# A planned attention and gated MLP kernel: the normalization goes from either of two engines to VectorE alone, and the instruction lists are searched anew under another rule for the shared port

## The chip, the cores and the metric

The kernel runs on one core of one Trainium2 chip. A core has five engines that run beside each other, each through its own list of instructions in order: TensorE (PE in the rows; its weight loads are PEld), VectorE (DVE), ScalarE (ACT), GpSimd (POOL) and SyncE (SP), which here issues the transfers. They wait for each other on semaphores. The metric is the device time of one execution in microseconds.

## The reference

Attention with 4 sink positions and a window of 128, over 4 batches of 8 heads, 768 positions, 64 values a head; its output goes through a gated MLP that mixes positions.

```python
scores = q @ k.T / sqrt(64)                      # kept: first 4 positions, and 0 <= i - j < 128
a = softmax(scores);  x = a @ v                  # [4, 768, 512] over all heads
h = relu(x @ w_in);  u, vv = h[..., :512], h[..., 512:]
v_n = (vv - mean(vv)) / sqrt(var(vv) + 1e-6)     # over the 512 features
v_s = einsum('ts,bsd->btd', w_spatial, v_n) + b_spatial[None, :, None]
out = (u * v_s) @ w_out
```

## The kernel before

Each batch is cut into 6 tiles of 128 positions, each tile into two halves of 4 heads: 48 half tiles. A half tile goes through this sequence; the names are those of the profile's tiles, the lines those of the profile.

- TensorE makes the scores `sc` (L901); VectorE masks them into `pexp` and finds the maximum (L906); ScalarE takes the exponential (L911).
- The weights are split into two f16 numbers: a high part, a rounded copy (L609 on ScalarE, L614 on VectorE), and a low part, the difference (L625, "p low", on VectorE or GpSimd). Both are written to `p` and turned by a transposing transfer into `pT` (L975). TensorE multiplies with the values into `av` (L1017 to L1025). VectorE divides (L1031 to L1033) and `x` is split in the same way and turned into `xT`.
- The first four tiles of batch 0 are "crossed": they stay in f32 and are turned by TensorE (`pt`, L938).
- TensorE makes `ps_v` from `xT` and `w_in` (L648, crossed L1091); ScalarE takes relu into `vr` (L1104); VectorE takes the statistics (L1110 to L1114); GpSimd takes the power -1/2 of the variance (L1117, tile `rs`); and the normalization L1120, one `tensor_scalar` that subtracts the mean and multiplies by that root, runs on VectorE or GpSimd. Then `vr` is split into `vn` (high L609 or L614, low L625).
- After all tiles of a batch have `vn`, TensorE makes `ps_s` with w_spatial, VectorE gates it (L1173, L1177, L1185, tile `g`), and `ps_o` with `w_out` gives the output. `ps_u`, the other half of w_in, is made from `xT` at any time before.

The order is not written by hand. Each step is added as a piece to a `Plan` with a rank (a table `WHEN` of offsets for each kind of step), the engines that may do it with an assumed cost on each, the tiles that it reads and writes, and a flag `shared`. `Plan.order` is a list scheduler that runs while the kernel is built: it keeps a time at which each engine comes free, takes again and again the piece that could end first (ties by rank), picks the engine, and at last sorts all pieces by the start that it gave them. That sorted order is what is written into the engines' lists; on the chip only the lists and the semaphores are left. `GAP` spaces kinds of steps out. The method `beside` prices the port that VectorE and GpSimd share: pieces with `shared=True` take longer in the plan when the other engine is at work.

```python
        if e == "d" and shared:
            return d + min(d, max(free["p"] - t, 0.0))
```

Here `d` is a piece's cost, `t` its start, and `free["p"]` the time at which GpSimd comes free. Where the plan sees TensorE idle, `warm` (L550) puts matmuls without a use ahead of the next piece.

Of the kernel before, what the change touches and what calls it, by code (L numbers as in the profile page):

```python
# [13 lines left out]
ALU = mybir.AluOpType  # L14
# [199 lines left out]
def scale_from_high_word(nc, pool, top, name):  # L214
# [15 lines left out]
NS = 4  # L230
# [17 lines left out]
    "p cross": (-687.57,), "x cross": (45.68,), "x copy": (-530.15,), "pt copy": (-21.66,),  # L248
    "qk load": (-52.27, -22.45), "k sink": (-299.97, -241.1), "k copy": (596.81, -4.88), "score": (-460.83, -45.27),
    "mask": (-434.05, -132.56), "exp": (-231.67, 303.69), "p high": (441.41, -96.21), "turn high": (936.3, 182.28),  # L250
    "sink high": (86.75, 1307.65), "sink low": (617.97, -42.55), "p low": (9.93, 184.55),
    "turn low": (-277.66, 336.94), "av": (-267.85, -97.14), "divide": (-122.58, -1.13), "x high": (2.44, 222.74),
    "x low": (-647.02, -338.15), "x turn": (-365.59, 573.11), "v load": (-91.35, 1.12), "v sum": (-115.53, -183.64),
    "v max": (-417.04, -486.9), "v scale": (49.3, 574.51), "v sink": (-76.81, 48.39), "v high": (-585.85, -85.54),
    "v low": (-1194.79, 92.72), "ps_v": (-90.29, 124.42), "v relu": (447.33, 231.24), "icv": (340.13, -439.38),
    "icu": (18.96, -359.27), "v stats": (-316.16, 10.81), "v root": (-34.24, 24.3), "v norm": (43.93, 41),
    "vn high": (-784.06, -355.87), "vn low": (132.46, 27.81), "ps_u": (430.62, 636.6), "u relu": (24.49, 187.78),
    "ps_s": (111.73, -587.51), "gate": (-484.79, -130.08), "times": (64.03, 257.91), "g high": (403.16, 1442.73),
    "g low": (-262.53, 67.91), "ps_o": (-30.69, -432.82), "o copy": (502.59, -325.5), "o store": (409.39, 625.48),
    "w_in 1 load": (866.11, -447.38), "w_in 1": (-114.89, -221.77), "w_in 1 split": (308.49, 129.53),  # L260
    "w_in 0 load": (-50.92, 1059.89), "w_in 0": (157.5, -167.59), "w_in 0 split": (-824.82, 34.49),
    "w_sp load": (441.32, 71.67), "w_sp sum": (660.12, -208.54), "w_sp split": (-36.66, 542.23),
    "w_out load": (383.08, 214.87), "w_out": (194.27, 993.88), "w_out split": (-129.44, 578.24), "q 0": (-157.42,),
    "w 0": (-429.64,), "w 1": (-392.14,), "v 0": (-82.26,), "w 2": (-173.84,), "v 1": (-173.83,), "w 3": (-391.66,),
    "v 2": (-159.4,), "q 1": (-83.27,),
}
GAP = {"o": 4.275, "pace": 0.925, "pace 0": 9.634, "s": 0.598, "u": 3.332, "v sum": 0.483, "w_in 0": 13.729, "w_in 1": 10.370, "w_out": 0.000, "w_sp": 11.737}
# [23 lines left out]
class Plan:  # L291
# [213 lines left out]
def fast_path(tc, st, qk, v, vs, w_in, w_sp, b_sp, w_out, out):  # L505

    nc = tc.nc
    TC = 256
    VNS = 2.0 ** 10
    G_LOW = 11  # L510
    G_U, G_S, G_B = 2.0 ** -20, 2.0 ** -24, 2.0 ** -27
    G_WIDE = 2.0 ** G_LOW / (G_U * G_S)
    with (
# [88 lines left out]
        def high(name, step, b, kind, n, views, reads, writes, scale=None):  # L602
# [16 lines left out]
            plan.add(name, step, b, ENGINES[kind], costs(kind, n, pointer=scale is not None), f, reads, writes)  # L619
# [35 lines left out]
        vals = {}  # L655
# [31 lines left out]
        def decode(name, step, src, i, c, f0, top=None):  # L687
# [6 lines left out]
            def clamp(e):  # L694
# [12 lines left out]
                ci(), ci(), 0x07FFFFFF, 3, op0=ALU.bitwise_and, op1=ALU.logical_shift_left), [], [("w32", i)])  # L707
# [3 lines left out]
            plan.add(name, step, 0, "p", 1.22, lambda e: nc.gpsimd.tensor_tensor(  # L711
                out=ci(), in0=ci(), in1=tl("wtmp", i), op=ALU.add), [("wtmp", i)], [("w32", i)])

        def w_in_half(half):
            name, f0 = f"w_in {half}", 512 * half
            gap = GAP[name]
            key = ("in", half)
            mx = vals["mx", key] = small.tile([P, KC], F32, tag="mxw", name="mxw", bufs=3)
            for c in range(KC):
# [4 lines left out]
                ("s", key), scale_from_high_word(nc, scal, vals["r", key], f"win{half}")), 2.35)  # L724
# [591 lines left out]
```

## Time and profile before

| | us |
|---|---|
| median of 3 runs | 471.77 (469.93 to 471.91) |
| profiled execution, its own time | 468.96 |
| its span, first to last instruction | 466.9 |
| TensorE busy / VectorE busy / ScalarE busy / GpSimd busy | 427.9 / 343.6 / 223.4 / 179.6 |
| mean granted TensorE clock, share of full speed | 0.964 |

The busy times are sums over the whole span and the stages differ, so the rows below also cut the span into stretches. PEclk is the granted TensorE clock as a share of 2.4 GHz; a stretch at 1.2 GHz shows 0.5.

### The profile page before, as it was taken

Reading aid. Unit: us, or ns where it says so; the run is one execution under the profiler, and the core shown is the slowest. Engines: PE = TensorE matmul, PEld = TensorE weight load, DVE = VectorE, ACT = ScalarE, POOL = GpSimd, SP = SyncE. Lnnn points to the kernel's source line nnn. Section 1 sums busy time; section 2 is a strip of 40 time slices with the busy share of each in tenths; the row PEclk is TensorE's granted clock in tenths of the full one; section 3 lists DMA queues with packets and bytes.
Section 4 is the critical chain, followed back from the end, with each engine's and each line's share of the span. In section 5 each row is a group of like instructions: output and inputs, shape, how many; then the busy total and the mean of one; then the engine's idle time right before and its main releaser. Section 6 shows DMA issues by size and latency. Waiting matters only on the chain.

```text
span 466.9 us, 9659 instructions
## 1 busy us (share of the span) xinstructions
PE 427.9 (92%) x3571; PEld 301.0 (64%) x3571; DVE 343.6 (74%) x988; ACT 223.4 (48%) x509; POOL 179.6 (38%) x205
## 2 busy tenths in 40 slices
PE   5789999887899899898989999999799999999993
PEld 4557666654677577456567667656587867488761
DVE  4798878998798998987789737858795536366331
ACT  5797986663557746546555325434340212320110
POOL 4506438847849646522505305306830001110000
PEclk9899999987989899899999999999799999999998
DMA  6987239366989972599958034366336212400101
GB/s 253 354 254 252 69 105 239 77 162 171 203 165 187 188 184 46 160 231 188 226 115 187 36 102 114 86 155 104 75 80 93 69 46 46 90 1 0 48 31 67
DMA packets 130055, 61.39 MB, mean 131 GB/s; under 512 B 105296, under 2 KB 118352, under 8 KB 130000
## 3 DMA queue, kind: packets, MB, share of 16 engines
q1 hardware_dynamic: 129856, 60.69, 53.9%
q8 instruction: 30, 0.49, 0.5%
q14 instruction: 25, 0.20, 0.1%
q10 hardware_dynamic: 144, 0.00, 0.0%
HBM read 28.82 MB, written 6.29 MB: 75 GB/s over the span
## 4 chain that ended last, share of the span: by engine, by line
PE 47%; DVE 18%; issue 13%; POOL 12%; ACT 4%; DMA 3%; SPq 0%; POOLq 0%; ACTq 0%; DVEq 0%
PE ps_s L648 13%; PE ps_o L1200 9%; PE ps_u L648 6%; POOL vr L1120 5%; PE sc L901 5%; PE ps_v L648 5%; DVE pexp L906 2%; POOL p L625 2%; PE ps_v L1091 2%; PE av L1011 2%; DVE vn L614 2%; ACT pexp L911 2%; DVE x L625 2%; POOL rs L1117 1%; DMA out<-ob 1%
## 5 line engine op out<-in xcount | busy, mean ns | idle before, releaser
L911 ACT ACTIVATE pexp<-pexp,nm 128x260 f32<-128x260 f32 (+1 forms) x192 | 82.1, 484 | 62.5 <-DVE nm L906 62.1
L648 PE MATMUL ps_s<-wsp,vn 128*128 128x256 f16 x864 | 102.2, 276 | 4.1 <-ACT ob L1211 4.1
L648 PEld LDWEIGHTS <-vn 128*128 128x128 f16 x864 | 84.3, 99 | 20.3 <-issue 7.7
L625 POOL TENSOR_TENSOR p<-pexp,p 128x1024 f16<-128x1024 f32 (+2 forms) x45 | 61.9, 1383 | 35.1 <-ACT p L609 28.8
L648 PE MATMUL ps_u<-xT,win 128*128 128x256 f16 x576 | 69.8, 278 | 2.3 <-DVE allmax_r L676 1.4
L901 PE MATMUL sc<-kring,q 64*128 64x260 f32 (+1 forms) x384 | 62.2, 413 | 9.0 <-DVE nm L906 8.9
L1200 PE MATMUL ps_o<-wout,g 128*128 128x512 f16 x288 | 65.4, 379 | 0.7 <-DVE g L1173 0.7
L648 PEld LDWEIGHTS <-win 128*128 128x128 f16 x576 | 56.4, 100 | 14.0 <-issue 5.3
L648 PE MATMUL ps_v<-win,xT 128*128 128x512 f16 x240 | 57.3, 396 | 0.0
L901 PEld LDWEIGHTS sc<-kring,q 64*128 64x128 f32 x384 | 38.6, 195 | 23.2 <-DVE nm L906 13.4
L1117 POOL TENSOR_TENSOR rs<-rs,mhalf 128x1 f32<-128x1 f32 x24 | 16.3, 680 | 91.5 <-DVE rs L1114 89.2
L1211 ACT ACTIVATE ob<-ps_o,ico 128x512 f32<-128x512 f32 (+1 forms) x24 | 16.0, 667 | 69.7 <-PE ps_o L1200 69.6
L1200 PEld LDWEIGHTS <-g 128*128 128x128 f16 x288 | 27.8, 98 | 31.8 <-issue 1.9
L648 PEld LDWEIGHTS <-xT 128*128 128x128 f16 x240 | 23.5, 102 | 30.1 <-issue 6.3
L1173 DVE SCALAR_TENSOR_TENSOR g<-ps_s,b_bc 128x256 f32<-128x256 f32 x48 | 20.1, 419 | 28.5 <-PE ps_s L648 28.4
L1151 ACT ACTIVATE u<-ps_u 128x256 f32<-128x256 f32 x48 | 17.8, 376 | 33.5 <-PE ps_u L648 33.1
L1120 POOL TENSOR_SCALAR vr<-vr,mv,rs 128x512 f32<-128x512 f32 x14 | 31.4, 2243 | 1.1
L1023 PE MATMUL av<-vring,pT 128*128 128x65 f16 x296 | 31.8, 196 | 0.0
L1025 PE MATMUL av<-vring,pT 128*128 128x65 f16 x296 | 31.7, 196 | 0.0
L1024 PE MATMUL av<-vring,pT 128*128 128x65 f16 x296 | 31.7, 196 | 0.0
L1023 PEld LDWEIGHTS <-pT 128*128 128x128 f16 x296 | 27.9, 99 | 1.9 <-issue 0.7
L1024 PEld LDWEIGHTS <-pT 128*128 128x128 f16 x296 | 27.8, 99 | 0.9
(163 smaller groups left out, 702.0 us busy)
## 6 DMA issues: line engine op xcount, KB each, us to landing
vraw<-v_s SPq DMA_DIRECT2D x24, 260.0 KB, 4.0
kring<-qk_t SPq DMA_DIRECT2D x24, 256.0 KB, 3.7
q<-qk_t SPq DMA_DIRECT2D x24, 256.0 KB, 3.3
out<-ob SPq DMA_DIRECT2D x24, 256.0 KB, 2.2
dec<-w_in SPq DMA_DIRECT2D x8, 512.0 KB, 6.6
wsp<-w_sp_t SPq DMA_DIRECT2D x6, 384.0 KB, 5.1
dec<-w_out SPq DMA_DIRECT2D x4, 512.0 KB, 4.4
pT<-p SPq DMA_TRANSPOSE x80, 3.1
```

The lines of the kernel that those rows point to most:

```text
L625: eng[e].tensor_tensor(out=o, in0=x, in1=hi, op=ALU.subtract)
L648: nc.tensor.matmul(o, a, m, start=(i == 0), stop=(i == n - 1))
L901: nc.tensor.matmul(view(h + q)[0], tl("q", (b, t))[rows, hp, :], keys, start=True, stop=True)
L911: nc.scalar.activation(po, po, AF.Exp, bias=nm()[:, q:q + 1], scale=-1.0)
L1023: nc.tensor.matmul(o[:, h], ph, vh, start=(t < 2 and j == 0), stop=False)
L1024: nc.tensor.matmul(o[:, h], ph, vl, start=False, stop=False)
L1025: nc.tensor.matmul(o[:, h], pl, vh, start=False, stop=(j == nb - 1 and (t < 2 or h == HH - 1)))
L1117: nc.gpsimd.tensor_tensor(out=vals["rs", i], in0=vals["rs", i], in1=mhalf, op=ALU.pow)
L1120: eng[e].tensor_scalar(vr(), vr(), vals["mv", i][:, 0:1], vals["rs", i], op0=ALU.subtract, op1=ALU.mult)
L1151: plan.add("u relu", r, b, "a", 0.365, lambda e: nc.scalar.activation(tl("u", (b, c0))[:, d, :], tl("ps_u", i)[:, :TC], AF.Relu, scale=G_U ...
L1173: nc.vector.scalar_tensor_tensor(out=g(), in0=tl("ps_s", i)[:, :TC], scalar=G_S, in1=b_bc[:, t0:t0 + TC], op0=ALU.mult, op1=ALU.add)
L1200: nc.tensor.matmul(o, lead, wout[:, w, d, :], start=(d == 0 and j == 0), stop=(d == KC - 1 and j == 2))
```

## The change

`v norm` had two engines to choose from, and now has VectorE alone. Five more kinds of pieces get `shared=True` (the rounded copies, the shift of the decode, the bias, a scaled copy of w_out, the scaled copy `g high`, and the normalization itself). In `beside` a shared VectorE piece no longer pays at most its own length: it pays 0.9 of all that is left of GpSimd's current piece. A dozen assumed costs are set anew. With these, the tables `WHEN` and `GAP` are replaced whole. No instruction's shape is changed, and no data moves to another place; what differs is which engine does a piece and where it stands in its list.

```diff
 WHEN = {
-    "p cross": (-687.57,), "x cross": (45.68,), "x copy": (-530.15,), "pt copy": (-21.66,),
+    "p cross": (-463.47,), "x cross": (37.18,), "x copy": (-412.04,), "pt copy": (-12.77,), "qk load": (27.62, 80.81),
...
-GAP = {"o": 4.275, "pace": 0.925, "pace 0": 9.634, "s": 0.598, "u": 3.332, "v sum": 0.483, "w_in 0": 13.729, "w_in 1": 10.370, "w_out": 0.000, "w_sp": 11.737}
+GAP = {"o": 0.446, "pace": 0.422, "pace 0": 10.293, "s": 4.023, "u": 3.039, "v sum": 2.275, "w_in 0": 5.196, "w_in 1": 7.851, "w_out": 0.221, "w_sp": 5.631}
...
         if e == "d" and shared:
-            return d + min(d, max(free["p"] - t, 0.0))
+            return d + 0.9 * max(free["p"] - t, 0.0)
...
-            plan.add(name, step, b, ENGINES[kind], costs(kind, n, pointer=scale is not None), f, reads, writes)
+            plan.add(name, step, b, ENGINES[kind], costs(kind, n, pointer=scale is not None), f, reads, writes, shared=True)
...
-            plan.add("score", i, b, "PE", 1.16 if t else 0.7, product, [("q", (b, t))] + keys, banks)
+            plan.add("score", i, b, "PE", 1.05 if t else 0.75, product, [("q", (b, t))] + keys, banks)
...
-                plan.add("av", i, b, "PE", 0.113 * n + (0.5 if t > 1 else 0.1), product_f32,
+                plan.add("av", i, b, "PE", 0.225 * n + (0.25 if t > 1 else 0.0), product_f32,
...
-            plan.add("v root", r, b, "p", 0.5, root, [], [("st", i)])
-            plan.add("v norm", r, b, "dp", {"d": 0.46, "p": 0.66}, norm, [("st", i)], [("vr", i)])
+            plan.add("v root", r, b, "p", 0.57, root, [], [("st", i)])
+            plan.add("v norm", r, b, "d", 0.46, norm, [("st", i)], [("vr", i)], shared=True)
...
             plan.add("g high", r, b, ENGINES["g high"], costs("g high", TC), lambda e: scaled_copy(
-                e, g2()[:, 0], g(), 2.0 ** -G_LOW), [("g", i)], [("g2", i, 0)])
+                e, g2()[:, 0], g(), 2.0 ** -G_LOW), [("g", i)], [("g2", i, 0)], shared=True)
```

Three places show how the lists move. The first is GpSimd's list before, in batch 0, from the normalization of one tile to the low part of the weights (p low, `128x1024`) that stands behind the normalization of another.

```order
L1117 TENSOR_TENSOR rs<-rs,mhalf 128x1
L1120 TENSOR_SCALAR vr<-vr,mv,rs 128x512
L625 TENSOR_TENSOR p_0_133<-pexp,p_0_133 128x1024
L625 TENSOR_TENSOR p_0_133<-pexp,p_0_133 128x16
L1117 TENSOR_TENSOR rs<-rs,mhalf 128x1
L625 TENSOR_TENSOR vn<-vr,vn 128x512
L1120 TENSOR_SCALAR vr<-vr,mv,rs 128x512
L625 TENSOR_TENSOR p_1_134<-pexp,p_1_134 128x1024
```

Twice a `128x1024` subtraction is the next instruction behind a normalization. This is GpSimd's list of the changed kernel at a like place, the roots of three tiles.

```order
L1117 TENSOR_TENSOR rs<-rs,mhalf 128x1 x2
L625 TENSOR_TENSOR vn<-vr,vn 128x512
L625 TENSOR_TENSOR p_1_134<-pexp,p_1_134 128x16
L625 TENSOR_TENSOR p_1_134<-pexp,p_1_134 128x1024
L1117 TENSOR_TENSOR rs<-rs,mhalf 128x1
L1177 TENSOR_TENSOR g<-g,u 128x256
```

The normalizations are gone from it, and what follows a root is a small or a short piece. The second place is VectorE's list before, at the second of those normalizations; the first `vn` cast waits for GpSimd's normalization.

```order
L614 CAST p_1_134<-pexp 128x1024
L616 TENSOR_SCALAR vring<-vraw,v_scale 128x8x64
L614 CAST vn<-vr 128x512
L1031 TENSOR_SCALAR den<-av 128x8
L1032 RECIPROCAL den<-den 128x8
L1033 TENSOR_TENSOR x<-av,den 128x512
L625 TENSOR_TENSOR p_1_134<-pexp,p_1_134 128x16
L625 TENSOR_TENSOR vn<-vr,vn 128x512
```

This is VectorE's list of the changed kernel in batch 3, where two tiles are normalized one behind the other.

```order
L614 CAST p_0_133<-pexp 128x1024
L1110 BN_STATS st<-vr 128x6
L1112 BN_AGGR mv<-st 128x2
L1114 TENSOR_SCALAR rs<-mv 128x1
L1120 TENSOR_SCALAR vr<-vr,mv,rs 128x512 x2
L614 CAST vn<-vr 128x512 x2
L625 TENSOR_TENSOR vn<-vr,vn 128x512 x2
```

The cast `vn` now follows the normalization on its own engine. The third place is TensorE's list near the start, the crossed tiles before: scores, `av` and the first `ps_v` take turns.

```order
L901 MATMUL sc<-kring,q 128x260 x4
L1011 MATMUL av<-vraw,pT 128x65 x8
L1091 MATMUL ps_v<-w_167,xT_462 128x512
L1091 MATMUL ps_v<-w_176,xT_462 128x512
L1091 MATMUL ps_v<-w_198,xT_462 128x512
L1091 MATMUL ps_v<-w_187,xT_462 128x512
L938 MATMUL pt<-ident,pexp 128x128 x4
L901 MATMUL sc<-kring,q 128x260 x4
```

And this is the same stretch of the changed kernel, the half tiles of the crossed tiles up to the first `ps_v`.

```order
L1007 MATMUL av<-vsraw,p_0_133 128x260
L1011 MATMUL av<-vraw,pT 128x65 x8
L665 MATMUL ps_row<-ident,allmax_m 1x128
L954 MATMUL pt<-ident,p_1_134 16x128
L901 MATMUL sc<-kring,q 128x260 x4
L1007 MATMUL av<-vsraw,p_1_134 128x260
L1011 MATMUL av<-vraw,pT 128x65 x8
L672 MATMUL ps_col<-allmax_789,ones 128x1
L901 MATMUL sc<-kring,q 128x260 x4
L1091 MATMUL ps_v<-w_176,xT_599 128x512
```

The first `ps_v` stood behind the scores of the fifth half tile; it now stands behind those of the ninth, all eight crossed half tiles first. Counted over the engines' lists, GpSimd has 14 normalizations, 23 of p low at 1024 and none of `x` low before, and 0, 21 and 4 now; VectorE has 10, 11 and 20, and now 24, 13 and 16. The plan writes the pieces of all engines in one order. In it, the next VectorE piece behind a p low on GpSimd (1024 or 512 wide) is one that reads and writes SBUF alone (a rounded copy, a low part, the normalization, a `g` piece and the like) at 11 of 26 places before, and at 6 of 24 now. What stands behind the last scores on TensorE is nearly the same list as before.

## Rows read from the trace of the kernel before

**Rows 1.** Busy time by stage; the clock and transfers stand last in each row.

```profile
core 0: us, PE busy (x) PEld busy (x) DVE busy (x) ACT busy (x) POOL busy (x), PEclk, DMA share, GB/s
0.00:17.00 17.00, 9.80 (x63) 7.25 (x63) 10.42 (x37) 9.55 (x19) 9.07 (x38) 1.00 0.81 286
17.00:60.00 43.00, 40.92 (x260) 29.40 (x260) 37.17 (x137) 37.57 (x92) 16.17 (x21) 0.96 0.67 218
60.00:342.00 282.00, 259.70 (x2328) 180.15 (x2326) 234.92 (x659) 150.44 (x348) 144.85 (x135) 0.95 0.65 144
342.00:460.00 118.00, 117.48 (x926) 84.24 (x924) 60.35 (x158) 25.49 (x51) 9.50 (x12) 1.00 0.23 51
460.00:467.00 7.00, 0.00 (x0) 0.00 (x0) 0.74 (x2) 0.38 (x1) 0.00 (x0) 0.80 0.24 83
```

**Rows 2.** TensorE's waits from 60 to 342 us: total us, times, longest.

```profile
PE sc L901 <- DVE nm L906: 8.5, 7, 2.4
...
PE av L1017 <- DVE p L625: 2.4, 1, 2.4
```

**Rows 3.** TensorE in time around 124 us, with idle time and releaser.

```profile
124.35 2.14 PE L648 MATMUL ps_s<-wsp,vn 128*128 128x256 f16 x18
128.90 0.27 PE L1017 MATMUL av<-vsink,pT 96*128 96x260 f16 x1 [2.41 <-DVE p L625]
```

**Rows 4.** Busy time in two stretches around that wait, columns as in rows 1.

```profile
126.00:129.00 3.00, 0.59 (x6) 0.32 (x4) 2.93 (x6) 0.21 (x1) 1.43 (x1) 1.00 0.45 162
129.00:133.00 4.00, 4.00 (x41) 3.05 (x40) 4.00 (x14) 3.52 (x8) 0.81 (x1) 0.59 0.93 117
```

**Rows 5.** GpSimd in time, 114 to 128 us.

```profile
114.54 2.60 POOL L1120 TENSOR_SCALAR vr<-vr,mv,rs 128x512 f32<-128x512 f32 x1
...
122.65 2.75 POOL L1120 TENSOR_SCALAR vr<-vr,mv,rs 128x512 f32<-128x512 f32 x1
125.38 2.05 POOL L625 TENSOR_TENSOR p<-pexp,p 128x1024 f16<-128x1024 f32 x1
```

**Rows 6.** VectorE in time in the same stretch.

```profile
114.66 0.69 DVE L614 CAST p<-pexp 128x1024 f16<-128x1024 f32 x1
...
122.43 0.79 DVE L614 CAST p<-pexp 128x1024 f16<-128x1024 f32 x1
...
125.44 2.27 DVE L614 CAST vn<-vr 128x512 f16<-128x512 f32 x1 [1.82 <-POOL vr L1120]
...
128.67 0.17 DVE L625 TENSOR_TENSOR p<-pexp,p 128x16 f16<-128x16 f32 x1
```

**Rows 7.** The chain of waits from 60 to 342 us, shares by line.

```profile
by line: issue 20.7%; POOL vr L1120 7.6%; PE ps_s L648 6.7%; PE sc L901 5.2%; POOL p L625 3.8%; PE ps_o L1200 3.7%; DVE pexp L906 3.5%; DVE vn L614 3.3%; DVE x L625 2.6%; PE ps_v L648 2.3%; POOL rs L1117 2.2%; DMA out<-ob 2.1%; DVE vsink L8
```

**Rows 8.** By tile: count, then duration in ns, least/median/greatest.

```profile
L1120 POOL TENSOR_SCALAR vr<-vr,mv,rs x14: 2071/2078/2755, 38.4 to 332.7; 128x512 f32<-128x512 f32 x14
L614 DVE CAST vn<-vr x14: 426/526/2278, 117.2 to 413.8; 128x512 f16<-128x512 f32 x14
L1120 DVE TENSOR_SCALAR vr<-vr,mv,rs x10: 542/546/2268, 66.5 to 413.2; 128x512 f32<-128x512 f32 x10
L625 DVE TENSOR_TENSOR x<-x,x x20: 677/691/2540, 86.2 to 396.7; 128x512 f16<-128x512 f32 x20
```

**Rows 9.** Groups by line and shape: busy us, mean ns, idle before.

```profile
L625 DVE TENSOR_TENSOR x<-x,x 128x512 f16<-128x512 f32 x20 | 20.1, 1007 | 0.7 <-POOL x L618 0.4
...
L614 DVE CAST vn<-vr 128x512 f16<-128x512 f32 x14 | 14.1, 1010 | 13.3 <-POOL vr L1120 13.1
...
L625 DVE TENSOR_TENSOR p<-pexp,p 128x1024 f16<-128x1024 f32 x11 | 13.7, 1241 | 0.1
...
L616 DVE TENSOR_SCALAR vring<-vraw,v_scale 128x512 f16<-128x512 f32 x13 | 6.1, 493 | 4.1 <-PE av L1025 4.1
```

**Rows 10.** Crossed `ps_v` in the chain of waits: start, length (us).

```profile
32.44 3.49 PE ps_v L1091 x8
...
52.16 3.44 PE ps_v L1091 x8
```

More of the change, by code (lines that the diff above doesn't have):

```diff
@@ L247 @@
 WHEN = {
-    "p cross": (-687.57,), "x cross": (45.68,), "x copy": (-530.15,), "pt copy": (-21.66,),
[L249 to L262, printed above, removed]
@@ L263 @@
-    "w_out load": (383.08, 214.87), "w_out": (194.27, 993.88), "w_out split": (-129.44, 578.24), "q 0": (-157.42,),
-    "w 0": (-429.64,), "w 1": (-392.14,), "v 0": (-82.26,), "w 2": (-173.84,), "v 1": (-173.83,), "w 3": (-391.66,),
-    "v 2": (-159.4,), "q 1": (-83.27,),
+    "p cross": (-463.47,), "x cross": (37.18,), "x copy": (-412.04,), "pt copy": (-12.77,), "qk load": (27.62, 80.81),
+    "k sink": (-1265.13, 104.01), "k copy": (1027.62, 30.74), "score": (-293.87, -87.66), "mask": (-569.68, -239.03),
@@ new lines @@
+    "exp": (-634.67, 808.04), "p high": (720.35, 12.02), "turn high": (1064.07, 324.41),
+    "sink high": (-226.41, 321.96), "sink low": (1193.15, 285.79), "p low": (8.77, 523.02),
+    "turn low": (-58.83, -13.88), "av": (-442.88, -275.38), "divide": (-115.55, 272.28), "x high": (-0.1, 227.04),
+    "x low": (-660.57, -237.49), "x turn": (-483.18, 614.2), "v load": (41.52, -24.87), "v sum": (-65.63, -332.06),
+    "v max": (-330.92, -514.68), "v scale": (76.16, 725.38), "v sink": (-187.98, -157.05),
@@ new lines @@
+    "v high": (-793.18, -91.53), "v low": (-1369.63, -23.34), "ps_v": (-16.36, 369.67), "v relu": (842.89, -264.63),
+    "icv": (362.96, -678.96), "icu": (-27.18, -350.17), "v stats": (-661.98, 102.13), "v root": (63.18, -272.42),
+    "v norm": (226.43, 511.61), "vn high": (-707.79, 74.9), "vn low": (197.01, -136.51), "ps_u": (1001.89, 408.24),
+    "u relu": (168.52, 254.14), "ps_s": (162.18, -524.45), "gate": (-535.26, -88.95), "times": (199.34, 393.2),
+    "g high": (280.49, 1526.6), "g low": (-455.93, 37.4), "ps_o": (-66.37, -161.59), "o copy": (486.93, -365.12),
@@ new lines @@
+    "o store": (-207.96, 765.9), "w_in 1 load": (11.93, -684.46), "w_in 1": (-166.94, -359.53),
+    "w_in 1 split": (607.72, -344.83), "w_in 0 load": (59.71, 1218.5), "w_in 0": (167.24, 327.78),
+    "w_in 0 split": (-597.61, -151.86), "w_sp load": (169.08, 71.79), "w_sp sum": (898.55, -272.36),
+    "w_sp split": (-211.46, 256.73), "w_out load": (530.5, 325.36), "w_out": (187.77, 716.58),
+    "w_out split": (-915.03, 463.68), "q 0": (-217.71,), "w 0": (-464.18,), "w 1": (-253.4,), "v 0": (55.57,),
```

17 lines of the change are left out of this document (9 added, 8 removed).

## The prediction

> **What bounds the kernel now.** I read the busy time by stage first. From 342 to 460 us TensorE is busy for 117.48 of 118 us at the full clock, and the last 7 us are the way out of the last tile: nothing there can be had by another order, since TensorE's work stays the same. From 17 to 60 us TensorE is busy for 40.92 of 43, with ScalarE at 37.57. What is left is the stage from 60 to 342 us: TensorE works for 259.70 of 282 us, so 22.3 us are idle, and the clock's mean there is 0.95, so about 0.05 x 282 = 14 us more are lost to stretches at 1.2 GHz [rows 1]. Some 36 us are to be had at most, and the last scores fall at the end of this stage; the 125 us behind them are fixed. VectorE is the busiest of the others, 234.92 of 282 us or 83%, ScalarE 53%, GpSimd 51% [rows 1].
>
> The waits of TensorE say who is late: the largest is for VectorE's masks, 8.5 us in 7 waits [rows 2]. One stall can be followed whole. TensorE sat idle for 2.41 us before the `av` at 128.90, until VectorE's small low part at 128.67 [rows 3, 6]; in the 4 us that came next the mean clock was 0.59, which costs 4 x 0.41 = 1.6 us more [rows 4]. So a stall of this size costs about 4 us, and 36 us are some nine of them.
>
> Why VectorE was late stands two rows up. GpSimd's normalization ends at 125.40; at 125.38 by the rows, that is at once, its next instruction starts, a p low of 2.05 us. VectorE's cast of `vn` waited for that same normalization and starts at 125.44, 60 ns behind the p low [rows 5, 6]. It takes 2.27 us, where the least of these casts took 0.426 [rows 8]: it is held until p low ends. So a collision costs 2.278 - 0.426 = 1.85 us. The normalization on GpSimd thus sets up the collision: it releases VectorE's cast at the very moment at which GpSimd goes on to its next piece. The chain of waits runs over L1120 on GpSimd for 7.6% of the 282 us, 21.4 us, more than over any other engine's line [rows 7].
>
> **The change part by part.** *The normalization.* VectorE takes 14 more at the median 0.546 us, +7.6 us; GpSimd loses 14 at 2.078 us or more, at least 29 us [rows 8]. GpSimd is busy for half of the stage, so what counts there is not its time but what it blocks.
>
> Does the normalization itself hold VectorE? Beside the two that ran 2.60 and 2.75 us, VectorE's casts of `p` took 0.69 and 0.79 us; it was the normalization that got longer, from 2.07 [rows 5, 6, 8]. So nothing is to be gained from lifting it off the port, only from not releasing the cast beside a p low. The Trainium skill, page "SBUF — State Buffer", section "Who interferes with whom", says that the pair of ports which VectorE and GpSimd share is an exclusive lock, held for a whole instruction by the one that starts first. The p low agrees with it, the normalization does not; by the page alone, the 14 normalizations would free up to 14 x 2.078 = 29 us of lock, by the rows none.
>
> *Other pieces that change engine.* VectorE gets 2 more p low at 1.241 us, +2.5; it loses 4 low parts of `x` at 0.691, -2.8, and 6 scaled copies `vring` at 0.493, -3.0 [rows 8, 9]. The other kinds move by one to six pieces each and cancel to within 0.3 us by their rows in the same view. VectorE's work is then +7.6 + 2.5 - 2.8 - 3.0 = +4.3 us, nearly all of it ahead of the last scores. ScalarE gets the scaled copies and a few rounded ones; at 53% in the stage it has room, and I cost them at nothing there. If that cover is gone (it is not there before 60 us, at 87%), each costs its length.
>
> *The collisions.* The casts of `vn` paid 14 x (1.010 - 0.426) = 8.2 us for them, the low parts of `x` 20 x (1.007 - 0.677) = 6.6 us, the two costliest forms [rows 8, 9]. In the new order the places where a VectorE piece that works from SBUF alone comes directly behind a p low of GpSimd fall from 11 to 6: 5 x 1.85 = -9.3 us. Bounds: the order is one thing and the moment another, so none may go (0); at most both forms lose all that they pay, -14.8. I take -9.3, since the casts behind a GpSimd normalization are gone as a pattern. The new pattern that could replace it is a normalization on VectorE released by the root on GpSimd just as a p low follows: one of the ten before paid for that, 2.268 against 0.546 us [rows 8], and in the new GpSimd list a root is mostly followed by a small piece. VectorE's sum is then +4.3 - 9.3 = -5.0 us, with ends of +4.3 and -10.5.
>
> *The latency.* Where a normalization is on the chain, 2.078 us become 0.546: of 21.4 us at most 21.4 x (1 - 0.26) = 15.8 go [rows 7, 8]. The least is nothing, where another chain lies close beside. The root stays on GpSimd, and now a semaphore stands between it and the normalization; the cast behind it needs none across engines, so I put the exchange at nothing.
>
> *The early crossed tiles.* Two crossed `ps_v` of 3.5 us each stood in the stretch from 17 to 60 us [rows 10], and now come behind all eight half tiles. If the stretch gets shorter by that, nothing is lost. ScalarE's 37.57 of 43 us lets it shrink by 5.4 at most [rows 1]; the 1.6 us that remain of 7.0 find room in 22.3 us of later idle time. I put it at nothing, with the other end below.
>
> *Sum.* VectorE's -5.0 us and the chain's 0 to -15.8 are two views of the same stalls and are not added. I take -6, one and a half stalls of 4 us: the first figure with a little of the second, near its low end because `issue`, the masks and the transfers have their own shares in the chain [rows 7]. The profiled execution took 468.96 us of its own, 2.8 below the median of 471.77 (its span is 466.9); 468.96 - 6 = 463.0, a ratio of 0.987, and on the median 465.6. I say 465.5.
>
> **The rivals.** *More comes back.* If the casts and the normalizations were the head of most stalls, the chain's whole 15.8 us go and with them the slow clock behind: 471.77 - 16 = 456. For it: the share in the chain. Against it: the other shares.
>
> *No change.* The collisions move to other pieces: the 6 places left, and four new low parts of `x` on GpSimd, which also read two tiles. -9.3 becomes about -4.3 and cancels with the work: 471.8.
>
> *Slower, VectorE becomes the bound.* At 83% it has the least room in the stage. Its +4.3 us of work come surely, the -9.3 depend on moments. If the collisions do not fall, +4.3 and one new stall of 4 us give 480. It decides as soon as VectorE's time above its least durations falls by less than 4.3 us. The Trainium skill, page "Perfetto Trace Analysis", section "Optimizing Scalar/DVE Operations", speaks for this rival: with VectorE saturated, work may be better moved off it, GpSimd included, though it warns that the shared port may undo that. The change does the opposite.
>
> *Slower, the crossed tiles.* Without `ps_v` between them the half tiles have only their own chain (scores, mask, exponential, turn, copy, `av`). If that chain does not get faster, the stretch stays 43 us, TensorE idles 7 us more in it, and the `ps_v` are paid later: at most +7, with some filled later about +5, 477. It decides when TensorE's busy time in the first 60 us falls with no earlier ninth score.
>
> **How the numbers follow.** Chances: the forecast, 2.4 to 11 us faster, 0.42 (its own range 460.5 to 469.5); more than that 0.14; no change 0.18; VectorE the bound 0.14; the crossed tiles 0.12. A measurement of this kernel can tell about 0.5%, 2.4 us, from no change. Faster 0.42 + 0.14 = 0.56, same 0.18, slower 0.26. The range for 8 in 10 goes from 455, which leaves out the best half of the first rival, to 477, which leaves out the VectorE rival and half of the other slow one's upper side.
>
> **What would show it.** Right: the casts of `vn` on VectorE with a mean near 0.5 us instead of 1.01; VectorE's waits at p low fewer by about five; TensorE's idle time in the middle stage below 20 us and its clock above 0.95; L1120 nearly gone from the chain; and the stage behind the last scores as long as before, 118 us. Wrong: normalizations on VectorE with a mean far above 0.55 us (held by a p low behind the root), the first 60 us with less TensorE work and no gain in time, or new waits of TensorE for `pT` or `x` that make up the stalls that went.

## The result, and the profile after

The changed kernel takes 441.55 us (median of 4, 440.75 to 443.53) against 470.85 (469.84 to 471.91) for the kernel before on the same chip: a ratio of 0.938, 95% interval [0.934, 0.943], 29 us or 6.2% faster. I had said 465.5, with a range down to 455. The sign was right, the size was far off. The profiled execution has a span of 439.9 us, 27.0 less than the 466.9 of before. Runs more than 1.5% above the fastest of their kernel are left out of all ratios below, but not of the medians.

The first lines of its page give the busy time of each engine, with the share of the span and the instructions.

```profile
span 439.9 us, 9637 instructions
PE 412.7 (94%) x3569; PEld 293.1 (67%) x3569; DVE 333.4 (76%) x991; ACT 230.6 (52%) x520; POOL 146.0 (33%) x190
```

TensorE does the same products (3569 and 3571 instructions) in 412.7 us of busy time, where it took 427.9; of this 15.2 us the larger part is the slow clock: at mean clocks of 0.964 and 0.986 some 17 us of the span were lost to it before and some 6 now. The rest of the span, in which it is idle, went from 39.0 to 27.2 us: 11.8 more. The stages show where; columns as in [rows 1], cut near the last scores.

```profile
0.00:17.00 17.00, 8.00 (x56) 6.27 (x56) 8.05 (x26) 6.44 (x10) 7.81 (x34) 0.92 0.76 253
17.00:60.00 43.00, 41.11 (x278) 31.57 (x279) 38.74 (x147) 38.48 (x98) 14.81 (x23) 0.91 0.76 248
60.00:316.00 256.00, 247.15 (x2317) 171.86 (x2317) 227.45 (x673) 162.40 (x366) 113.14 (x123) 1.00 0.75 156
316.00:433.00 117.00, 116.42 (x924) 83.38 (x920) 58.42 (x148) 22.93 (x47) 10.26 (x12) 1.00 0.21 51
433.00:440.00 7.00, 0.00 (x0) 0.00 (x0) 0.74 (x2) 0.39 (x1) 0.00 (x0) 0.82 0.24 83
```

The last scores start and last as follows, first in the kernel before, then in the changed one:

```profile
342.49 1.75 PE L901 MATMUL sc<-kring,q 64*128 64x260 f32 x8 [0.34 <-DVE nm L906]
```

```profile
315.62 1.15 PE L901 MATMUL sc<-kring,q 64*128 64x260 f32 x8
```

They end at 316.8 us, where they ended at 344.2, some 2 us behind the cut at 342. What stands behind them takes 123.1 us, where it took 122.7. The middle stage, as cut, is 256 us long, where it was 282. TensorE is idle for 8.85 us of it, where it was for 22.3, and its mean clock there is 1.00, where it was 0.95. VectorE is at 89% of the middle stage, and still TensorE hardly waits for it: its waits there (total us, times, longest) begin with

```profile
PE ps_v L1091 <- ACT xT L1069: 1.9, 2, 1.3
PE av L1023 <- DVE x L1033: 1.8, 1, 1.8
PE ps_row L665 <- DVE allmax_m L662: 1.6, 2, 0.9
PE sc L901 <- DVE nm L906: 1.3, 1, 1.3
```

The scores waited 8.5 us for masks in [rows 2]; now it is 1.3. The chain of waits over the same stretch, by line:

```profile
by line: PE ps_s L648 10.1%; PE ps_o L1200 9.8%; PE ps_u L648 9.6%; DMA pT<-p 8.3%; PE sc L901 6.8%; DVE pexp L906 6.3%; PE ps_v L648 6.2%; DVE vring L633 3.4%; issue 3.1%; PE ps_v L1091 2.8%; DMA vraw<-v_s 2.2%; PE av L1023 2.1%; PE av L10
```

TensorE's own products head it, `issue` has 3.1% where [rows 7] have 20.7%, and L1120 is not among the lines shown. The tiles of the normalization (count, then least/median/greatest ns), for [rows 8]:

```profile
L1120 DVE TENSOR_SCALAR vr<-vr,mv,rs x24: 536/541/1467, 71.3 to 386.2; 128x512 f32<-128x512 f32 x24
L614 DVE CAST vn<-vr x12: 416/427/490, 100.6 to 386.8; 128x512 f16<-128x512 f32 x12
```

No cast of `vn` is held any longer: the greatest is 490 ns, where it was 2278. To see all collisions, I took for each VectorE instruction its time above the least of its shape, and put it down to the GpSimd instruction that ran beside it; such a case is called a hold below. Beside p low (1024 or 512 wide) this was 25.2 us in 18 cases before, and is 15.9 us in 12 cases now: 9.3 us less, the very figure of the prediction. Other forms pay part of it now, though. The low parts of `x` have a mean of 0.885 us, where [rows 9] have 1.007; the scaled copies `vring` have 0.813, where they had 0.493, and their second form, L633, has 0.875:

```profile
L633 DVE SCALAR_TENSOR_TENSOR vring<-vraw,v_scale,vring 128x512 f16<-128x512 f32 x21 | 17.9, 875 | 0.0
L625 DVE TENSOR_TENSOR x<-x,x 128x512 f16<-128x512 f32 x16 | 14.2, 885 | 0.1
L616 DVE TENSOR_SCALAR vring<-vraw,v_scale 128x512 f16<-128x512 f32 x7 | 5.7, 813 | 1.4 <-PE av L1025 1.4
```

In the kernel before, L633 had 0.747:

```profile
L633 DVE SCALAR_TENSOR_TENSOR vring<-vraw,v_scale,vring 128x512 f16<-128x512 f32 x21 | 15.3, 747 | 0.0
```

VectorE's whole busy time fell by 10.2 us, from 343.6 to 333.4.

### The profile page after: what moved, and what is told of

It reads as the page before. It is cut to its first block, busy times and chain, and to the rows that moved or that the text cites. A ratio compares the mean times of both kernels' runs of the same rounds, so it can differ in the third digit from the quotient of the medians.

```text
span 439.9 us, 9637 instructions
## 1 busy us (share of the span) xinstructions
PE 412.7 (94%) x3569; PEld 293.1 (67%) x3569; DVE 333.4 (76%) x991; ACT 230.6 (52%) x520; POOL 146.0 (33%) x190
## 4 chain that ended last, share of the span: by engine, by line
PE 63%; DVE 18%; DMA 8%; ACT 5%; POOL 2%; issue 2%; SPq 1%; DVEq 0%; ACTq 0%; POOLq 0%
PE ps_s L648 17%; PE ps_o L1200 13%; PE ps_u L648 10%; PE ps_v L648 7%; PE sc L901 5%; DMA pT<-p 5%; DVE pexp L906 4%; PE av L1011 2%; DVE vring L633 2%; DMA dec<-w_in 2%; PE ps_v L1091 2%; ACT pexp L911 2%; PE av L1023 1%; PE av L1025 1%; PE av L1024 1%
## 5 line engine op out<-in xcount | busy, mean ns | idle before, releaser
L648 PE MATMUL ps_s<-wsp,vn 128*128 128x256 f16 x864 | 99.5, 273 | 0.0
L648 PEld LDWEIGHTS <-vn 128*128 128x128 f16 x864 | 83.6, 98 | 14.5 <-issue 2.7
L625 POOL TENSOR_TENSOR p<-pexp,p 128x16 f16<-128x16 f32 (+2 forms) x49 | 58.4, 1198 | 63.7 <-ACT p L609 50.3
L648 PE MATMUL ps_u<-xT,win 128*128 128x256 f16 x576 | 67.4, 273 | 0.1
L648 PEld LDWEIGHTS <-win 128*128 128x128 f16 x576 | 54.8, 98 | 11.4 <-issue 3.9
L901 PE MATMUL sc<-kring,q 64*128 64x260 f32 (+1 forms) x384 | 56.2, 401 | 5.2 <-DMA q<-qk_t 3.3
L648 PE MATMUL ps_v<-win,xT 128*128 128x512 f16 x240 | 54.5, 379 | 0.0
L901 PEld LDWEIGHTS sc<-kring,q 64*128 64x128 f32 x384 | 35.2, 193 | 17.5 <-DVE nm L906 4.2
L648 PEld LDWEIGHTS <-xT 128*128 128x128 f16 x240 | 22.9, 98 | 26.9 <-issue 1.4
L1117 POOL TENSOR_TENSOR rs<-rs,mhalf 128x1 f32<-128x1 f32 x24 | 17.9, 746 | 67.0 <-DVE rs L1114 65.8
L1023 PE MATMUL av<-vring,pT 128*128 128x65 f16 x296 | 30.8, 193 | 1.8 <-DVE x L1033 1.8
L1025 PE MATMUL av<-vring,pT 128*128 128x65 f16 x296 | 30.5, 193 | 1.0 <-DMA pT<-p 1.0
L1024 PE MATMUL av<-vring,pT 128*128 128x65 f16 x296 | 30.6, 193 | 0.2 <-DVE vring L633 0.2
L1023 PEld LDWEIGHTS <-pT 128*128 128x128 f16 x296 | 27.3, 97 | 4.0 <-issue 3.0
L609 ACT CAST p<-pexp 128x32 f16<-128x32 f32 (+2 forms) x48 | 24.4, 532 | 7.1 <-DMA pT<-p 6.7
```

What stands on the lines that cost most here:

```text
L609: nc.scalar.copy(o, x)
L625: eng[e].tensor_tensor(out=o, in0=x, in1=hi, op=ALU.subtract)
L648: nc.tensor.matmul(o, a, m, start=(i == 0), stop=(i == n - 1))
L901: nc.tensor.matmul(view(h + q)[0], tl("q", (b, t))[rows, hp, :], keys, start=True, stop=True)
L1023: nc.tensor.matmul(o[:, h], ph, vh, start=(t < 2 and j == 0), stop=False)
L1024: nc.tensor.matmul(o[:, h], ph, vl, start=False, stop=False)
```

## The experiments

**Theory 1**: VectorE pieces held by a long p low on GpSimd, those behind a GpSimd normalization first, start most of the stalls of TensorE. **Theory 2**: the new lists as a whole decide how much work TensorE has ahead, and with it whether a delay becomes a stall. **Theory 3**: only the sum of VectorE's own work counts. All times below are medians; the ratio is that to runs of the kernel before on the same chip.

| run | us | ratio, 95% interval |
|---|---|---|
| lists of before, normalization executed on VectorE | 458.0 | 0.974 [0.969, 0.979] |
| lists of before, pause behind the normalization | 465.2 | 0.988 [0.982, 0.994] |
| lists of before, p low in four parts | 464.7 | 0.989 [0.982, 0.996] |
| lists of before, normalization on VectorE and p low in parts | 449.6 | 0.955 [0.948, 0.963] |
| the changed kernel | 441.6 | 0.938 [0.934, 0.943] |
| new lists, 14 normalizations on GpSimd | 450.8 | 0.959 [0.954, 0.964] |
| new lists, five more holds | 446.0 | 0.950 [0.944, 0.955] |
| new lists, p low in four parts (second, longer measurement) | 435.8 | 0.929 [0.926, 0.932] |

**The normalization alone, on either list.** The first two runs leave each kernel's order in time as it is, and only execute 14 normalizations (the same tiles in both) on the other engine.

```diff
-                eng[e].tensor_scalar(vr(), vr(), vals["mv", i][:, 0:1], vals["rs", i], op0=ALU.subtract, op1=ALU.mult)
+                nc.vector.tensor_scalar(vr(), vr(), vals["mv", i][:, 0:1], vals["rs", i], op0=ALU.subtract, op1=ALU.mult)
```

> The kernel before with its own lists; only the 14 normalizations that ran on GpSimd run on VectorE, each at the place where the plan had put it. Theory 1 (the normalization on GpSimd, which releases VectorE's cast of vn just as a p low follows, starts most of TensorE's stalls): most of the gain comes back, 446 to 453 us. Theory 2 (the new lists as a whole keep TensorE supplied; which engine normalizes matters little): 463 to 470 us. Theory 3 (only VectorE's own time counts: +7.6 us of work against 8.2 us of collisions of the cast): 469 to 472 us.

In the other, `eng["p" if i in ON_GPSIMD else "d"]` stands there in the changed kernel, with the 14 tiles that had GpSimd before.

> The changed kernel with its own lists; only the same 14 tiles as before are normalized on GpSimd again. Theory 1: the stalls come back, 456 to 466 us. Theory 2: 441 to 448 us, since the lists stay. Theory 3: VectorE gets 7.6 us less to do and some collisions, 438 to 446 us.

458.0 and 450.8: both lie between the ranges of Theories 1 and 2. On the old lists VectorE gets 7.6 us more work and the kernel is 12 us faster (2.6%), so Theory 3 falls. On the new lists the engine is worth 2.05%, some 9.6 us. The other way round, the lists are worth 4.1% (19 us) with the normalization on GpSimd and 3.6% (17 us) with it on VectorE. 12.2 and 16.8 make up the 29.0 us on one path, 19.3 and 9.6 on the other. Neither theory has it alone. In the tile view of the first run most casts of `vn` are free, with 0.427 us at the median:

```profile
L614 DVE CAST vn<-vr x14: 414/427/1586, 119.8 to 405.3; 128x512 f16<-128x512 f32 x14
```

Beside p low, however, VectorE still pays 22.6 us in this run, where it paid 25.2: the holds fell by 2.6 us in sum, and the kernel's time by 12.

The third run keeps the normalization on GpSimd and only keeps GpSimd from going on at once: a small write behind each.

```diff
+        pause = const.tile([P, P], F16, name="pause")
...
+                if e == "p":
+                    nc.gpsimd.memset(pause, 0.0)
```

> The kernel before with its own lists and engines; behind each of the 14 normalizations on GpSimd stands a write of a scratch tile of 0.2 us, so that VectorE's cast of vn can start ahead of the next GpSimd piece. Theory 1: the cast is not held any more, its mean falls from 1.01 to about 0.5 us, and with it most stalls go, 446 to 455 us. Theory 2: the cast is not held, and the time falls by 2 to 8 us, 463 to 469 us. Theory 3: by the 6 to 8 us that the cast paid.

465.2, 5 us faster (1.2%), though the kernel now does more; this lies in the range of Theory 2. The tile view shows why: VectorE's cast gets in ahead of the p low (the added line shifts the numbers by one: L615 is L614, L1121 is L1120).

```profile
L615 DVE CAST vn<-vr x14: 426/427/832, 118.8 to 412.9; 128x512 f16<-128x512 f32 x14
L1121 POOL TENSOR_SCALAR vr<-vr,mv,rs x14: 2071/2077/2747, 40.8 to 332.1; 128x512 f32<-128x512 f32 x14
```

So the pattern followed in [rows 5, 6] is real, and to break it gives about 5 us, where the normalization on VectorE gives 12. The other 7 go with the normalization itself, 2.08 us against 0.55 on the chain; that is by subtraction, not measured by itself.

**What a hold costs.** In the changed kernel, five 2.08-us pieces on GpSimd were put behind the roots of five tiles, just as VectorE's normalization is released.

```diff
+HOLD = {(1, 0), (1, 2), (1, 4), (2, 1), (2, 3)}
...
+                if i in HOLD:
+                    wide = st.ident.unsqueeze(1).to_broadcast([P, 8, P])
+                    nc.gpsimd.tensor_tensor(out=rooms[:, NT].bitcast(F16)[:, :1024].rearrange("p (a b) -> p a b", b=P), in0=wide, in1=wide, op=ALU.subtract)
```

> The changed kernel with one more wide GpSimd piece (two inputs, 128x1024, into memory that nothing reads any more) right behind the root of five tiles, so that VectorE's normalization is held for it five times, 1.85 us each. Theory 1 (each such collision costs TensorE a stall of some 4 us): 455 to 463 us. Theory 2 (TensorE has work ahead in the new lists): 441 to 445 us. Theory 3: by VectorE's 9 us or less, 445 to 451 us.

446.0, 4.4 us more by the medians and 5.3 by the ratios. Only three of the five met a VectorE piece, for 3.8 us together, and only one of these was a normalization (0.85 us); the others were a cast and a low part of `p`. That is 1.5 to 1.8 us of the kernel for each hold that came about, below the 4 us of a stall. The time lies in Theory 3's range and just above Theory 2's, and with three holds in place of five the run does not decide between them. In the other direction every p low on GpSimd is issued in four parts of 256 columns, so that no single p low runs for 2 us.

```diff
+                if e == "p" and kind == "p low":
+                    for h in range(HH):
+                        nc.gpsimd.tensor_tensor(out=o[:, h], in0=x[:, h], in1=hi[:, h], op=ALU.subtract)
+                    return
                 eng[e].tensor_tensor(out=o, in0=x, in1=hi, op=ALU.subtract)
```

> The kernel before, its lists unmoved, but every p low on GpSimd is issued as four instructions of 256 columns instead of one of 1024; nothing is left out. No single instruction of GpSimd then holds VectorE for 2 us, so the 25.2 us that VectorE pays beside p low should fall to about a third. Theory 1 (a long p low beside VectorE's pieces starts most of the stalls, whatever the lists): 446 to 456. Theory 2 (the lists decide how much work TensorE has ahead, and with it what a delay costs): the holds get short, but the pieces stand where they stood, 460 to 467. Theory 3 (only the sum of VectorE's own work counts): 470, no change.

> The same four short p low, on the lists of before with the 14 normalizations executed on VectorE (the first experiment, 458.0). Nothing is left out. Theory 1: with both causes of long holds gone the old lists reach about the new ones' time, 441 to 449. Theory 2: the normalization already took the largest part; 453 to 458, and 12 us or more stay with the lists. Theory 3: 458.

> The changed kernel with the same four short p low; nothing is left out. It still pays 15.9 us of VectorE time beside p low. Theory 1: that should go to about 5 and TensorE get back a few us, 436 to 439. Theory 2: TensorE has work ahead in the new lists, so that nothing comes back: 440 to 443. Theory 3: 441.5, no change.

464.7, 449.6 and 438.1. The tile view of the first of them has the parts:

```profile
L627 POOL TENSOR_TENSOR p<-pexp,p x104: 403/655/1713, 63.8 to 340.6; 128x256 f16<-128x256 f32 x92, 128x128 f16<-128x128 f32 x12
```

Four parts of 0.655 us at the median take GpSimd 2.6 us where one p low took 2.05, and VectorE pays less all the same: 14 to 15 us beside p low on the old lists, where it was 25.2. This is more than the third that I had expected, because some 36 short holds came in place of 18 long ones. The gain is 1.1% alone and 1.9% (9 us) once the normalization is on VectorE too. On the old lists both causes together bring 20.5 of the 29 us; 449.6 lies 0.6 us above the range of Theory 1 and 3.4 below that of Theory 2. The third run was measured a second time.

> The changed kernel with p low on GpSimd in four parts, once more and with more runs: 438.1 before, a ratio of 0.930 against 0.938 for the changed kernel. If the short holds give something back in the new lists too: 436 to 439.5. If not: 440 to 442.

435.8, a ratio of 0.929 [0.926, 0.932], which lies below the changed kernel's [0.934, 0.943]: a version faster than both, by some 4 us (0.9%), with 4 to 5 us of VectorE time left beside p low.

**What a stall costs.** TensorE is made to wait six times in the last batch for small GpSimd writes that themselves wait for TensorE. The long stalls have ten writes, as shown; the short ones have four, `range(4)`.

```diff
+                if b == B - 1 and d % 2 == 0:
+                    for k in range(2):
+                        nc.tensor.matmul(tl("ps_s", i)[:, :P], late, late, start=True, stop=True)
+                        if k == 0:
+                            for _ in range(10):
+                                nc.gpsimd.memset(late, 0.0)
```

> The changed kernel, in which TensorE is made to wait six times, ahead of an s product of the last batch, for ten small writes of GpSimd (about 0.2 us each, so some 2.2 us) that themselves wait for a small product of TensorE; nothing is left out. This asks what a stall costs. If the price in the prediction holds (2.4 us idle and 1.6 us of slow clock behind it, 4 us), six stalls of some 2.3 us cost about 22 us: 464. If only the idle time is lost and the clock stays up, about 14 us: 455. If TensorE makes up for a stall later, because the others get ahead meanwhile, less than 8 us: under 450.

> The changed kernel with six stalls of TensorE as in the experiment with the long ones, but with four small writes of GpSimd in each, not ten, so some 1.5 us idle instead of 2.75; nothing is left out. The long ones cost 4.6 us each, and the clock stood at half speed for 3.4 us behind five of six. If the clock drops behind a short stall as well: 6 x (1.5 + 1.7) = 19 us, 460 to 462. If it stays up: 6 x 1.6, so 450 to 452, and a stall that gets shorter gains more than its own length.

The long ones, in time on TensorE (L650 is the L648 of before), and the clock behind one of them (columns as in [rows 1]):

```profile
397.54 0.22 PE L1166 MATMUL ps_s<-late 128*128 128x128 f16 x1
400.51 0.23 PE L1166 MATMUL ps_s<-late 128*128 128x128 f16 x1 [2.75 <-POOL late L1169]
400.58 4.67 PE L650 MATMUL ps_s<-wsp,vn 128*128 128x256 f16 x26
```

```profile
401.00:404.00 3.00, 3.00 (x17) 2.13 (x16) 0.00 (x0) 0.00 (x0) 0.00 (x0) 0.50 0.00 0
```

And the short ones:

```profile
396.54 0.22 PE L1166 MATMUL ps_s<-late 128*128 128x128 f16 x1
397.93 0.23 PE L1166 MATMUL ps_s<-late 128*128 128x128 f16 x1 [1.17 <-POOL late L1169]
398.00 4.09 PE L650 MATMUL ps_s<-wsp,vn 128*128 128x256 f16 x36
```

```profile
398.00:401.00 3.00, 3.00 (x29) 2.70 (x30) 0.80 (x2) 0.00 (x0) 0.00 (x0) 1.00 0.00 0
```

Six waits of 2.75 us lengthened the span by 467.2 - 439.9 = 27.3 us, 4.6 each, and behind five of the six the granted clock was 0.5 (1.2 GHz), so that 17 products were done in 3 us and not 29. The runs of this kernel differ more than most: those in its ratio lie between 463.4 and 469.5 us, which makes 3.6 to 4.7 us each. Six waits of 1.17 us cost 450.5 - 439.9 = 10.6 us, 1.8 each, and the clock stayed at 1.00 behind all six. In both, 0.3 us of each is the two small products that the run adds. So a price of about 4 us holds for a wait of 2.75 us at this place, and a wait of less than half of that costs some 0.4 of it.

The length of a wait does not settle the clock by itself, as the trace of the kernel before shows. Behind a wait of 1.32 us the clock fell:

```profile
192.53 1.75 PE L901 MATMUL sc<-kring,q 64*128 64x260 f32 x8 [1.32 <-DVE nm L906]
194.50:198.00 3.50, 3.50 (x28) 1.81 (x24) 3.43 (x15) 2.77 (x5) 2.50 (x1) 0.51 1.00 281
```

Behind one of 2.23 us it did not:

```profile
213.62 3.54 PE L648 MATMUL ps_s<-wsp,vn 128*128 128x256 f16 x31 [2.23 <-ACT ob L1211]
213.60:218.00 4.40, 4.38 (x48) 3.95 (x48) 3.29 (x12) 2.88 (x8) 1.62 (x4) 1.00 0.75 188
```

**The tables and the rules.** Three runs have the planner write new lists, with one half of the change each: the new tables under the old rules (`WHEN` and `GAP` alone put into the kernel before); the changed kernel with the old price in `beside`; and the kernel before with `v norm` for VectorE alone.

```diff
-            return d + 0.9 * max(free["p"] - t, 0.0)
+            return d + min(d, max(free["p"] - t, 0.0))
```

> The kernel before with the changed kernel's tables (WHEN and GAP) and nothing else of the change: the planner may again choose GpSimd for the normalization, prices the port as before and has the old durations, and writes its lists anew from the new tables. Nothing is left out. If the tables carry the order that keeps TensorE supplied by themselves: 442 to 452, the new lists' gain with a normalization on GpSimd here and there. If tables and rules make a good list only together, so that another list comes out: 460 to 480. By VectorE's own work alone (Theory 3): 468 to 472.

> The changed kernel, in which only the price of the shared port in the planner goes back to the old one (a VectorE piece is delayed by at most its own length); tables, durations and the normalization on VectorE stay, and the lists are written anew. Nothing is left out. If the price with which the planner sees a p low beside VectorE is what keeps collisions out of the lists: the collisions come back, 446 to 456. If the tables carry the order: 440 to 445. If any deviation from what the tables were searched with spoils the list: 460 or more.

> The kernel before, whose planner is told that the normalization is VectorE's alone and shares the port; the old tables, the old price and the old durations stay, and the lists are written anew. Nothing is left out. In the first experiment the same 14 normalizations went to VectorE without a new list: 458.0. If the engine of the normalization is what counts: 452 to 459. If the gain beyond it lies in lists that are searched for this very plan: at 458 or above, up to 475, since the old tables were not searched for it.

478.0 (ratio 1.020 [1.013, 1.027], slower than before), 464.3 (0.985 [0.980, 0.990]) and 457.0 (0.974 [0.968, 0.980]). The last agrees with 458.0: the normalization on VectorE is worth its 12 us on another list too. The tables carry nothing by themselves, and the one line of the old price loses 22 of the 29 us by the ratio; its ten runs spread from 459.0 to 467.8. In the first of the three, between 60 and 200 us, TensorE is idle for 16.2 us at a mean clock of 0.91:

```profile
60.00:200.00 140.00, 123.81 (x1014) 83.00 (x1014) 118.54 (x334) 89.61 (x200) 83.33 (x81) 0.91 0.67 148
```

**What the new lists have beyond both causes.** With short holds and the normalization on VectorE in both, the old lists stand at 0.955 and the new at 0.929, 12 us apart. The first guess was the masks: at 0.955 the scores still waited for them, 5.0 us in three waits. On VectorE's list each mask was put where the planner has its scores ready; TensorE's list did not move.

```diff
-            final.append((t, k, f, e))
+            final.append((ready[i] if e == "d" and [w[0] for w in ps[i][6]] == ["pexp", "nm"] else t, k, f, e))
```

> The lists of before, with the normalization on VectorE and p low in four short parts (449.6 so far), and one thing more: on VectorE's list each mask of the scores stands at the time at which the planner has its scores ready, not at the time at which it found VectorE free; the other lists keep their order. Nothing is left out. If what the new lists have beyond the two known causes is that their masks come in time for TensorE's next scores: the 5.4 us of waits of the scores go, with the slow clock behind them, 440 to 445. If masks ahead only make other pieces of VectorE late: 448 to 455.

> The same masks ahead on the lists of before with the normalization on VectorE, and p low whole (458.0 so far). Nothing is left out. If the masks are what was late: 447 to 452. If a long p low ahead of the mask is what made it late, whatever the list: 455 to 460.

> The changed kernel with its masks put ahead on VectorE in the same way; nothing is left out. If its masks already come in time: 440 to 444, or more where other pieces get late. If some of its 8 us of idle TensorE between 60 and 200 us is still due to masks: 436 to 439.

457.5, 462.5 and 446.3: each is slower than without, by 4 to 8 us of the medians and 7 to 10 of the ratios. So masks put ahead in this way are not what the new lists have. The waits of TensorE in the first, from 60 to 316 us, show what happened (its lines stand 4 further down: L1021 is L1017, L905 is L901):

```profile
PE av L1021 <- DVE x L1037: 4.5, 1, 4.5
PE sc L905 <- DVE nm L910: 3.4, 3, 2.0
PE ps_u L652 <- DVE allmax_r L680: 2.0, 2, 1.2
```

The scores wait for less, 3.4 us, and the `av` for 4.5 on an `x` that VectorE now does later. The second question was whether the other 138 pieces that change engine carry it, or the order in time. `ENGINE_OF` is a table from a piece's number to the engine that executes it, with 152 entries in the first run and 138 in the second.

```diff
-            final.append((t, k, f, e))
+            final.append((t, k, f, ENGINE_OF.get(ps[i][1], e)))
```

> The order in time of the lists of before, but each of the 152 pieces that the new lists give to another engine (the 14 normalizations and 138 more) is executed on that engine; TensorE's and the queues' order stay. Nothing is left out. With the normalizations alone this gave 458.0. If the choice of engines carries the rest: 442 to 452. If the order in time carries it: 455 to 465, since the other choices were made for another order.

> The order in time of the new lists, with the 138 other pieces on the engines of before; the normalization stays on VectorE. Nothing is left out. If the order in time carries the rest: 441 to 447. If the choice of engines carries it: 452 to 458. If order and engines belong together: both this run and the one beside it stand far above 441, at 450 to 465.

458.9 (0.976 [0.972, 0.980]) and 457.9 (0.975 [0.972, 0.979]). All 152 new engines on the old order bring no more than the 14 normalizations alone (0.974), and the new order with the other 138 pieces on their old engines loses 17 of the 29 us. Between 60 and 200 us the latter leaves TensorE idle for 15.6 us:

```profile
60.00:200.00 140.00, 124.37 (x1084) 83.59 (x1083) 131.34 (x356) 88.10 (x201) 75.78 (x76) 0.99 0.69 152
```

The changed kernel with short parts has 5.1 us there, in the best run of all:

```profile
60.00:200.00 140.00, 134.88 (x1281) 92.47 (x1280) 132.91 (x401) 108.66 (x242) 95.00 (x129) 1.00 0.87 180
```

So the rest belongs to order and engines together, and to no single kind of piece that I tried.

## Why the prediction was right in kind and wrong in size

- *Where the time can come from.* Right. Only the stage from 60 us to the last scores got shorter (282 to 256 us as cut); what stands behind is as long as before. Idle time and slow clock in the stage made up some 36 us, and 26 of them went.
- *The cost of the normalization on VectorE.* Right: 0.541 us at the median and 1.467 at most, where one of the ten before took 2.268.
- *The collisions, 5 x 1.85 = -9.3 us.* Right in sum, 25.2 to 15.9 us, but that it agrees to a tenth is luck. The casts of `vn`, with a mean of 0.43 us, pay nearly nothing of their 8.2 us, and the low parts of `x` pay 16 x (0.885 - 0.677) = 3.3 of their 6.6: together some 11 us less, of the 14.8 that the prediction gave as the most. `vring` and other forms pay some of it back, which the prediction did not have. VectorE's busy time, with ends of +4.3 and -10.5, came to -10.2, at its good end.
- *The price of a stall, about 4 us.* Right for waits of 2.75 us: 3.6 to 4.7 measured. That it falls to 1.8 at 1.17 us was not in the prediction, which took one price for all; so what shortens many stalls may give back their clock as well.
- *The sum.* This is the step that failed: "I take -6, one and a half stalls of 4 us". Measured were 27 us of span, between six and seven such stalls. The figure went wrong in two terms. First, the chain's "0 to -15.8" was not added, since I took it for another view of VectorE's -5.0; the engine alone, on the old lists, gave 12 us while VectorE's work rose by 7.6. VectorE's time is not what TensorE gains: what counts is which of its pieces is late, and 14 pieces of 2.08 us on the chain were. Second, the new order had no term at all. The prediction counts collisions in it and treats all else that moves as nothing; the lists alone gave 17 to 19 us. Of these, fewer and cheaper holds are about 4 to 5 by subtraction (short parts gain 9 us on the old list with the normalization on VectorE, and 4 on the new), and for some 12 no single cause was found.
- *The rival "more comes back", 456.* The first experiment, 458.0, comes near it: 12 of its 15.8 us are the engine's part of the gain. It lacked the lists' part just as the forecast did.
- *The rival "VectorE becomes the bound", 480.* It fell: VectorE went from 83% to 89% of the stage, and TensorE waits for it for less. The Trainium skill, page "Perfetto Trace Analysis", section "Optimizing Scalar/DVE Operations", says that with VectorE saturated it may make sense to move some work off it, GpSimd included. At 83 to 89% the first two experiments measure the opposite for the normalization, on either list, by 12 and 9.6 us. The section's own reservation, that such a move might not help since GpSimd shares a port with VectorE, fits the 25 us that VectorE paid beside p low.
- *The rival of the crossed tiles, 477.* The sign that it named came, its price did not show. TensorE's busy time in the first 60 us fell from 9.80 + 40.92 = 50.72 us to 8.00 + 41.11 = 49.11, at a lower mean clock between 17 and 60 us (0.91 for 0.96), and the scores of the ninth half tile come no earlier. They start at 47.15 us in the kernel before and at 48.55 in the changed one:

```profile
47.15 1.43 PE L901 MATMUL sc<-kring,q 64*128 64x260 f32 x8
```

```profile
48.55 1.15 PE L901 MATMUL sc<-kring,q 64*128 64x260 f32 x8
57.38 1.15 PE L901 MATMUL sc<-kring,q 64*128 64x260 f32 x8
58.45 1.98 PE L1091 MATMUL ps_v<-w,xT 128*128 128x512 f32 x4
```

The scores at 57.38 us are those of the eleventh half tile: the first `ps_v` stands behind the eleventh, and not behind the ninth as is said ahead of the prediction. It was near 32 us before [rows 10]. The stage behind the first 60 us got 26 us shorter all the same. What the early part lost was not measured by itself.
- *Whether the normalization holds the port.* The prediction took from [rows 5, 6, 8] that it does not, against the whole-instruction lock of the Trainium skill, page "SBUF — State Buffer", section "Who interferes with whom". For p low the lock agrees with what the parts did: shorter instructions, shorter holds. For the normalization the trace of the kernel before agrees with the prediction: beside all 14 of them VectorE paid 1.2 us in four cases. One stretch has both kinds. The copy `vring` runs beside a normalization and takes its usual 0.49 us, and the normalization its usual 2.08; then the cast of `vn` starts beside a p low and takes 2.27.

```profile
322.82 2.08 POOL L1120 TENSOR_SCALAR vr<-vr,mv,rs 128x512 f32<-128x512 f32 x1
324.87 2.06 POOL L625 TENSOR_TENSOR p<-pexp,p 128x1024 f16<-128x1024 f32 x1
```

```profile
323.45 0.49 DVE L616 TENSOR_SCALAR vring<-vraw,v_scale 128x512 f16<-128x512 f32 x1
324.94 2.27 DVE L614 CAST vn<-vr 128x512 f16<-128x512 f32 x1 [1.00 <-POOL vr L1120]
```

What stays open: which property of the new lists is worth the last 12 us. The gain of the new lists is lost by the tables under the old rules and under the old price, by the engines without the order and the order without the engines, and in part by moving one kind of piece. That the lists were fitted as a whole to this kernel's durations is an argument, and no run shows it.

## What to carry to other kernels

When work moves from GpSimd to VectorE, don't price it in VectorE's busy time: look at which VectorE piece the GpSimd piece released, and at what GpSimd does next beside it. A long GpSimd instruction that holds VectorE, as p low does here, can be cut into parts; this made GpSimd's own work longer and the kernel faster on the old list and on the new. A list that was searched anew as a whole needs a term of its own with wide ends: the collisions that could be counted in it, 9.3 us of VectorE's time, stand against 29 us of the kernel.

## What the runs showed of the hardware that I had not expected

- In the last batch, behind 1.17-us waits of TensorE the granted clock stayed at 1.00 six times of six, and behind 2.75-us waits it went to 0.5 five times of six. Length alone does not decide: in the kernel before it fell behind a wait of 1.32 us and not behind one of 2.23.
- A p low of GpSimd in four parts takes 4 x 0.655 = 2.6 us for 2.05 whole, and its holds of VectorE add up to 14 to 15 us where they were 25.2.
- A GpSimd normalization of 2.08 us ran beside VectorE's `vring` without holding it (0.49 us); a GpSimd p low of 2.06 us held the cast of `vn` to 2.27.
- A 0.2-us write on GpSimd behind a 2.08-us normalization was enough for VectorE's cast to go first: 0.427 us at the median and 0.832 at most, where it had been up to 2.278.
